# A new written order for the start of attention and a feed-forward layer, with head 18 in it

## The chip, the cores and the metric

The kernel runs on one core of a Trainium2 chip. The metric is the device time of one execution in microseconds (us). Shown are the median of three timed executions and one profiled execution. Its engines are named as the profile names them: PE is TensorE (PEld its weight loads), DVE VectorE, ACT ScalarE, POOL GpSimd, SP the queue that issues all DMA transfers.

## The reference, cut to what matters

Eight batches of eight heads, 576 tokens of 64 elements. A query sees only keys of a short window behind it (32 keys, plain in heads 0 to 3 of a batch, every fourth key in heads 4 to 7). The attention's output, 4608 tokens of 512, goes through two matrices with a clipped square between them.

```
scores = scale * np.matmul(q, k.transpose(0, 1, 3, 2))
scores = np.where(masks, scores, -1e9)
attn = np.exp(scores - max) ; attn = attn / (sum + 1e-09)
x = np.matmul(attn, v)                    # heads side by side: 4608 x 512
h = x @ w_in                              # 512 -> 2048
g = np.where(h >= 1, h, np.where(h <= -1, 0.0, (h + 1) ** 2 / 4))
return g @ w_out                          # 2048 -> 512
```

## The kernel before

A head's 576 queries are six tiles of 96, each with a band of 128 keys. Tokens go through the feed-forward layers in nine groups of 512 with sixteen slices of the inner 2048 each, so in 144 steps: step s is a first layer "A" (four parts of three products), an elementwise chain, and a second layer "B" (four parts of three products). B runs two steps behind A. Products of 512 columns are made of a high and a low part, hence three of each.

The first batch and a half (heads 0 to 17, steps 0 to 17) stand in a table, `OPENING`: a list of tokens that `play` (L588) turns into one instruction or a few each. On each engine and on SP the instructions keep the order of the table. From head 18 and step 18 on a loop makes the order (L642), and it is the same loop before and after. The tokens that matter here:

- `q8`, `k8`, `v8`: loads of queries, keys, values (two heads at a time for heads 0 to 15, one head from head 16 on); `wi3`, `wo3`: loads of a slice of a weight matrix. SP issues them one after the other, and one that waits for its place to come free holds up those behind it.
- `S0.2`: score product of head 0, tile 2 (L287; from head 16 on L302, two tiles, split into high and low parts). Heads 0 to 15 put four tiles, then two, in one PSUM bank.
- `r0.2`: the DVE instruction that adds the mask and takes the row minimum (L263); `m` its mask part from head 16 on (L326). `e0.2`: exponential on ACT (L354), or of a whole head in one instruction after `z`, a subtraction on POOL (L351, L360). Which heads go which way stands in `whole_pass` (L344). `u`, `i`, `R`, `n`: sum, guard, reciprocal, normalisation; `n` runs on POOL or, for the heads in `by_vector`, on DVE (L390).
- `T`, `p`: transposes on PE and their copies; `V`, `x`, `l`: product with the values, its high part (ACT) and low part (DVE).
- `awi3`, `bwi3`, `jwi3`, `hwi3`, `lwi3`: a weight slice is unpacked (a, b on ACT, j on DVE, L188) and split (h on ACT, l on POOL, L199).
- `A4.1`, `B4.1`: products of the layers (L522, L561). `y`, `s`, `j`, `g`, `d`: the chain between them (DVE, ACT, DVE, ACT, DVE). Only two banks hold A's results, so A of a step waits for `d` of the step two before.
- `cq18`, `ck18`, `cs18`, `cl18`: splits of queries and keys of a head from 16 on, on ACT, ACT, DVE and POOL (L217, L220, L224, L228). Raw and split queries and keys have one place each: `q18`'s load waits for `cq17` and `cs17`, `k19`'s for `ck18` and `cl18`, and `cq18` and `ck18` wait for the last score product of head 17.
- `W3`: three products on a constant, to no result.

After the table the loop begins with the score product S18.0, then A of step 18.

Of the kernel before, what the change touches and what calls it, by code (L numbers as in the profile page):

```python
# [60 lines left out]
z8 awi4 wo11 jwo1 A0.2 bwi4 A0.3 lwi3 wi6 e8 S10.0 l6.1.1 y0 hwo1 S11.0 S10.1 S11.1 S10.2 r10.0 wi13 S11.2 s0
r11.0 S10.3 S11.3 r11.1 A1.2 lwo1 r10.1 e11.0 r11.3 r10.2 awi5 j0 wo8 A1.3 e11.1 z9 r10.3 r11.2 g0 S10.4 y1
S11.4 wi8 S10.5 bwi5 S11.5 d0 s1 r10.5 A2.0 r11.4 e11.3 wi10 jwi4 e11.4 A2.1 u8 e9 wo4 A2.2 hwi4 r10.4 jwi5
z10 i8 A2.3 awo2 j1 q14 hwi5 B0.0 R8 u9 g1 B0.1 bwo2 lwi4 k12 d1 B0.2 e11.2 i9 jwo2 e10 B0.3 n8 A3.0 awi7 R9
r11.5 hwo2 y2 A3.1 bwi7 u10 A3.2 s2 n9 A3.3 jwi7 e11.5 i10 B1.0 i11 lwi5 B1.1 j2 hwi7 B1.2 R11 g2 y3 T9.1 lwo2
# [5 lines left out]
V10.1 lwi10 x10.0.0 B4.0 bwo10 l10.0.0 s6 lwi9 jwo10 B4.1 awo8 B4.2 x10.1.1 bwo8 B4.3 j6 awi11 A7.0 l10.1.1
hwo10 jwo8 A7.1 x10.1.0 lwo10 g6 l10.1.0 A7.2 bwi11 d6 hwo8 S12.4 jwi11 S13.4 S12.5 S13.5 awo9 A7.3 lwo8 r13.4
hwi11 r12.5 r12.4 B5.0 r13.5 bwo9 y7 B5.1 lwi11 awi12 jwo9 B5.2 s7 bwi12 S12.0 S13.0 S12.1 S13.1 awo7 r12.0
S12.2 S13.2 r12.1 S12.3 jwi12 S13.3 hwo9 B5.3 q16 r13.0 bwo7 lwo9 j7 A8.0 e13.0 r13.2 g7 jwo7 A8.1 e13.5 A8.2
e13.2 r12.3 awi14 r13.1 A8.3 r12.2 d7 e13.4 z12 B6.0 e13.1 r13.3 y8 bwi14 B6.1 e13.3 jwi14 B6.2 hwo7 i13 e12
# [10 lines left out]
p15.1 S16.0 g14 S16.4 m16.0 A15.0 m16.4 r16.1 A15.1 r16.0 e16.1 d14 S16.2 e16.0 A15.2 r16.4 ck17 m16.2 r16.5
A15.3 cq17 r16.2 cl17 r16.3 e16.2 B13.0 cs17 e16.3 B13.1 e16.4 e16.5 B13.2 k18 i16 V14.1 y15 V14.0 R16 x14.1.1
s15 n16 l14.1.1 B13.3 x14.1.0 j15 x14.0.1 x14.0.0 A16.0 l14.0.1 g15 l14.1.0 A16.1 l14.0.0 t16.1.1 A16.2
t16.0.0 t16.0.1 A16.3 t16.2.1 t16.2.0 t16.1.0 S17.2 B14.0 y16 m17.2 B14.1 s16 d15 B14.2 j16 B14.3 A17.0 g16
# [632 lines left out]
```

## Time and profile before

| what | value |
|---|---|
| median of 3 timed executions | 933.76 us (933.42 to 936.98) |
| the profiled execution's own time | 932.25 us |
| its span in the trace | 930.5 us |
| PE busy | 908.0 us (98%) |
| DVE, ACT, POOL busy | 675.6, 497.4, 233.2 us |
| mean granted PE clock | 0.99 of full |
| chain that ended last | PE 93%, DVE 3%, ACT 2%, DMA 1% |

The span is what the profiler saw from the first to the last instruction; the execution's own time is 1.75 us longer. A busy PE is one with an instruction in it, at whatever clock was granted.

### The profile page before, as it was taken

The numbers are of one execution on the slowest core, as the hardware profiler recorded it, in microseconds if no ns is written. First come the engines' busy times: TensorE is split into PE (matmuls) and PEld (weight loads), VectorE is DVE, ScalarE is ACT, GpSimd is POOL, SyncE is SP. The second block draws the span as 40 slices with busy tenths as digits, with TensorE's granted clock in tenths as the row PEclk, the third lists the DMA queues.
The fourth block names the chain that finished last, engine by engine and source line by source line (L and its number), as shares of the span: only waits on it lengthen the run. The fifth ranks groups of instructions, "written<-read, shape, count | busy, mean of one in ns | idle before, by whom it ended". The sixth has DMA issues, their size and how long they took to land.

```text
span 930.5 us, 14387 instructions
## 1 busy us (share of the span) xinstructions
PE 908.0 (98%) x4856; PEld 743.1 (80%) x4856; DVE 675.6 (73%) x1967; ACT 497.4 (53%) x1372; POOL 233.2 (25%) x150
## 2 busy tenths in 40 slices
PE   8899996999999999999999999999999999999998
PEld 6677885788888888888888888888888888888886
DVE  5998777688888888888887888888888643334333
ACT  6999964455565556555655555555655322222222
POOL 1585542122222222222222222222222000000000
PEclk8999999899999999999999999999999999999999
DMA  9882022122232113222322123222321010001001
GB/s 349 301 331 88 6 74 86 56 70 70 70 115 63 49 57 114 70 70 70 96 89 61 57 67 115 70 70 70 115 69 45 1 46 1 1 1 45 1 1 45
DMA packets 31018, 73.86 MB, mean 79 GB/s; under 512 B 3520, under 2 KB 3808, under 8 KB 30944
## 3 DMA queue, kind: packets, MB, share of 16 engines
q1 hardware_dynamic: 30944, 72.94, 23.6%
q8 instruction: 38, 0.62, 0.3%
q14 instruction: 36, 0.29, 0.1%
HBM read 63.49 MB, written 9.44 MB: 78 GB/s over the span
## 4 chain that ended last, share of the span: by engine, by line
PE 93%; DVE 3%; ACT 2%; DMA 1%; issue 0%; POOL 0%; SPq 0%; DVEq 0%; ACTq 0%
PE acc L561 42%; PE h L522 42%; PE s L302 4%; PE o L456 3%; PE s L287 1%; DVE c_place L263 1%; PE t L432 1%; DVE c L263 0%; DMA msk<-mask_in 0%; DVE xl L497 0%; DMA qr<-q_in 0%; ACT xh L492 0%; DVE wo_m L188 0%; DVE pt L401 0%; DMA out<-out 0%
## 5 line engine op out<-in xcount | busy, mean ns | idle before, releaser
L561 PE MATMUL acc<-wo,gh 128*128 128x512 f32 x1152 | 384.4, 394 | 0.0
L522 PE MATMUL h<-xh,wi 128*128 128x512 f32 x1152 | 358.1, 392 | 0.6 <-DVE gl L549 0.5
L561 PEld LDWEIGHTS acc<-wo,gh 128*128 128x128 f32 x1152 | 216.5, 188 | 47.3
L522 PEld LDWEIGHTS h<-xh,wi 128*128 128x128 f32 x1152 | 210.2, 189 | 39.5 <-DVE gl L549 1.3
L561 PE MATMUL acc<-wo,gl 128*128 128x512 f32 x576 | 225.2, 391 | 0.0
L522 PE MATMUL h<-xl,wi 128*128 128x512 f32 x576 | 225.0, 391 | 0.0
L228 POOL TENSOR_TENSOR kk<-kr,kk 128x608 fp32r<-128x608 f32 x48 | 94.1, 1960 | 425.7 <-ACT kk L220 425.7
L354 ACT ACTIVATE c<-c 96x128 f32<-96x128 f32 x318 | 124.4, 392 | 119.1 <-DVE c L263 118.9
L535 ACT ACTIVATE y<-y,consts 128x512 f32<-128x512 f32 x144 | 104.1, 723 | 125.9 <-DVE y L532 125.7
L545 ACT CAST gh<-h 128x512 fp32r<-128x512 f32 x144 | 84.5, 587 | 121.8 <-PE acc L561 117.5
L532 DVE TENSOR_SCALAR y<-h 128x512 f32<-128x512 f32 x144 | 99.2, 689 | 60.3 <-PE h L522 59.9
L538 DVE TENSOR_TENSOR h<-h,y 128x512 f32<-128x512 f32 x144 | 100.4, 698 | 49.0 <-ACT y L535 47.8
L522 PEld LDWEIGHTS h<-xl,wi 128*128 128x128 f32 x576 | 108.6, 188 | 23.4
L549 DVE TENSOR_TENSOR gl<-h,gh 128x512 fp32r<-128x512 f32 x144 | 98.6, 685 | 38.1 <-ACT gh L545 38.0
L561 PEld LDWEIGHTS acc<-wo,gl 128*128 128x128 f32 x576 | 108.2, 188 | 19.6
L401 DVE STREAM_TRANSPOSE pt<-c 32x192 f32<-32x192 f32 x288 | 106.0, 368 | 8.0 <-POOL c L390 4.7
L390 POOL TENSOR_TENSOR c<-c 96x768 f32<-96x768 f32 x56 | 82.5, 1475 | 31.5 <-DVE c L385 31.4
L326 DVE TENSOR_TENSOR c<-s,msk 96x256 f32<-96x256 f32 (+1 forms) x168 | 61.4, 377 | 37.0 <-PE s L302 36.0
L263 DVE CUSTOM_DVE_ANT_0 c<-s,c 96x128 f32<-96x128 f32 x288 | 70.5, 280 | 1.0
L302 PE MATMUL s<-kk,qs 128*96 128x256 f32 x288 | 57.8, 284 | 8.4 <-DVE qs L224 8.4
L302 PEld LDWEIGHTS s<-kk,qs 128*96 128x96 f32 x288 | 46.2, 162 | 24.1 <-issue 9.0
L354 ACT ACTIVATION_READ_ACCUMULATOR c<-c 96x1 f32 x318 | 59.6, 187 | 0.0
(74 smaller groups left out, 634.2 us busy)
## 6 DMA issues: line engine op xcount, KB each, us to landing
kr<-k_in SPq DMA_DIRECT2D x53, 304.0 KB, 3.1
qr<-q_in SPq DMA_DIRECT2D x53, 288.0 KB, 2.7
vt<-v_in SPq DMA_DIRECT2D x29, 384.0 KB, 3.9
out<-out SPq DMA_DIRECT2D x36, 256.0 KB, 2.1
wi_raw<-w_in SPq DMA_DIRECT2D x16, 512.0 KB, 9.0
wo_raw<-w_in SPq DMA_DIRECT2D x16, 512.0 KB, 8.7
v_place<-v_in SPq DMA_DIRECT2D x3, 384.0 KB, 7.2
k_place<-k_in SPq DMA_DIRECT2D x3, 304.0 KB, 6.6
```

Source lines behind the costliest of these rows:

```text
L228: nc.gpsimd.tensor_tensor(out=kk[:, 1], in0=kr, in1=kk[:, 0].bitcast(F32), op=ALU.subtract)
L302: PE.matmul(out=split_view(n, t0)[:, t - t0], lhsT=hd["qs"][:, t * QT : (t + 1) * QT], rhs=hd["ks"][:, :, t * QT : t * QT + 128], start=Tr ...
L354: nc.scalar.activation(out=c[:, t], in_=c[:, t], func=AF.Exp, bias=st[:, 0, t : t + 1], scale=-1.0, **total)
L390: engine.tensor_tensor(out=c, in0=c, in1=spread(factor(n)), op=ALU.mult)
L401: nc.vector.transpose(out=pts[n % 2][r : r + 32, :, 32 * g : 32 * g + 32], in_=heads[n]["c"][32 * g : 32 * g + 32, :, r : r + 32],)
L522: PE.matmul(out=hps[s], lhsT=ready[f"wi{f}"][:, w, 128 * c : 128 * c + 128], rhs=x[:, c], start=c == 0 and i == 0, stop=c == NC - 1 and i ...
L532: nc.vector.tensor_scalar(out=y, in0=hps[s], scalar1=-1.0, scalar2=1.0, op0=ALU.max, op1=ALU.min)
L535: nc.scalar.activation(out=ys[s], in_=ys[s], func=AF.Square, bias=half_t, scale=0.5)
L538: nc.vector.tensor_tensor(out=hps[s], in0=hps[s], in1=ys.pop(s), op=ALU.max)
L545: nc.scalar.copy(out=gs[s][0], in_=hps[s])
L549: nc.vector.tensor_tensor(out=gl, in0=hps.pop(s), in1=gh.bitcast(F32), op=ALU.subtract)
L561: PE.matmul(out=acc[m], lhsT=g[:, r], rhs=w[:, part], start=f == 0 and i == 0, stop=f == NF - 1 and i == 2,)
```

## The change

The table is written anew. All loads, weight conversions and the order of heads against steps move. A bank's score products now all precede the first minimum taken from that bank; before, they alternated. Head 18's queries are loaded, and split, before the last steps of the table; before, they stood at its very end. Exponentials of heads 4 and 6 become whole passes (with `z4`, `z6` on POOL), head 9's go back to single tiles; `n5` goes from DVE to POOL. There are three constant products less. The mask and the identity matrix for transposes come in one array and one transfer, and the first pair's queries and keys come in halves.

```diff
 OPENING = """
-k0 q0 msk q4 q2 k2 v0 k4 k6 S0.0 q6 S1.0 S0.1 S1.1 r0.0 S0.2 wi0 r0.1 S1.2 e0.0 S0.3 r1.0 S1.3 S0.4 r0.2 wi3
+k0 q0 msk Q0 K0 q2 k2 S0.0 q4 S1.0 S0.1 S1.1 S0.2 k4 S1.2 wi1 S0.3 r0.0 r0.1 e0.0 e0.1 q6 S1.3 r1.0 r1.2 r0.2
...
-S17.0 d16 A17.1 m17.0 A17.2 r17.2 r17.0 e17.2 A17.3 r17.1 r17.3 e17.0 B15.0 e17.1 y17 e17.3 B15.1 s17 B15.2
-j17 B15.3 S17.4 g17 m17.4 ck18 r17.5 r17.4 d17 e17.5 cl18 e17.4 i17 R17 n17 k19 q18 cq18 cs18 q19
+s16 B14.3 j16 S17.2 A17.0 cq18 m17.2 r17.2 A17.1 ck18 r17.3 cs18 g16 A17.2 cl18 e17.2 d16 A17.3 e17.3 B15.0
+i17 y17 B15.1 R17 s17 n17 k19 B15.2 q19 j17 B15.3 g17 d17
 """
-    msk = const.tile([QT, 3, 128], F32, name="msk")
-    ident = const.tile([QT, QT], F32, name="ident")
+    fixed = const.tile([QT, 3 * 128 + QT], F32, name="fixed")
+    msk = fixed[:, : 3 * 128].rearrange("p (k j) -> p k j", k=3)
+    ident = fixed[:, 3 * 128 :]
...
+    first_q, first_k = 3 * QT, 3 * QT + 32
+    whole = {}
+
+    def rest_q(n):
+        nc.sync.dma_start(out=whole["q", n][:, first_q:], in_=q[n // 2][:, first_q:])
+
+    def rest_k(n):
+        nc.sync.dma_start(out=whole["k", n][:, first_k:], in_=k[n // 2][:, first_k:])
...
-            nc.sync.dma_start(out=qr, in_=q[n // 2])
+            some = slice(0, first_q if n == 0 else S)
+            nc.sync.dma_start(out=qr[:, some], in_=q[n // 2][:, some])
+            whole["q", n] = qr
...
-    whole_pass = (8, 9, 10, 12, 14)
-    sum_apart = (4, 5, 6, 7)
-    by_vector = (3, 5, 7)
+    whole_pass = (4, 6, 8, 10, 12, 14)
+    sum_apart = (5, 7)
+    by_vector = (3, 7)
...
         if token == "msk":
-            nc.sync.dma_start(out=msk, in_=mask.rearrange("k p j -> p k j"))
-        elif token == "id":
-            nc.sync.dma_start(out=ident, in_=eye)
+            nc.sync.dma_start(out=fixed, in_=fixed_in)
```

**Where head 18 comes in, on SP.** `kr18`, `qr18` are head 18's raw keys and queries, `out0_0` to `out0_3` the first four results. Before:

```order
L149 DMA kr18_1670<-k2_in 128x608
L574 DMA out<-out0_0_1778 128x512
L574 DMA out<-out0_1_1788 128x512
L574 DMA out<-out0_2_1795 128x512
L574 DMA out<-out0_3_1802 128x512
L149 DMA kr19_1824<-k2_in 128x608
L135 DMA qr18_1826<-q2_in 128x576
L135 DMA qr19_1830<-q2_in 128x576
```

After:

```order
L163 DMA kr18_1649<-k2_in 128x608
L147 DMA qr18_1657<-q2_in 128x576
L588 DMA out<-out0_0_1788 128x512
L588 DMA out<-out0_1_1797 128x512
L163 DMA kr19_1803<-k2_in 128x608
L588 DMA out<-out0_2_1808 128x512
L147 DMA qr19_1811<-q2_in 128x576
L588 DMA out<-out0_3_1817 128x512
```

Head 18's queries moved from behind head 19's keys to right behind its own keys.

**The same place on PE.** `s17_4` and `s17_2` are head 17's score products, `s18_0` head 18's first, `acc0` the second layer, `h1` the first. Before:

```order
L561 MATMUL acc0_3_764<-wo15_1351,gh15_1706 128x512
L561 MATMUL acc0_3_764<-wo15_1351,gl15_1707 128x512
L561 MATMUL acc0_3_764<-wo15_1351,gh15_1706 128x512
L302 MATMUL s17_4_1805<-kk17_1645,qs17_1644 96x256 x2
L302 MATMUL s18_0_1842<-kk18_1813,qs18_1812 96x256 x2
L522 MATMUL h1_2_1848<-xh1_384,wi2_486 128x512 x2
```

After (between the two score products stand the 24 products of A17 and B15, of which four rows are shown):

```order
L316 MATMUL s17_2_1754<-kk17_1615,qs17_1614 96x256 x2
L536 MATMUL h1_1_1757<-xh1_409,wi1_461 128x512 x2
L536 MATMUL h1_1_1757<-xl1_410,wi1_461 128x512
...
L575 MATMUL acc0_3_757<-wo15_1350,gl15_1714 128x512
L575 MATMUL acc0_3_757<-wo15_1350,gh15_1713 128x512
L316 MATMUL s18_0_1834<-kk18_1762,qs18_1761 96x256 x2
L536 MATMUL h1_2_1840<-xh1_409,wi2_522 128x512 x2
```

Before, head 17's last score product stood directly ahead of head 18's first; now a whole step stands between.

**PE at the first pair of heads.** `s0_0` and `s1_0` are the banks of heads 0 and 1, `s2_0` and `s3_0` those of the next pair; what each instruction waits for is in brackets (DVE: a minimum). Before:

```order
L287 MATMUL s0_0_93<-kr0_75,qr0_77 96x128 [waits DMAHW1_49,DMAHW0_49]
L287 MATMUL s1_0_107<-kr0_75,qr0_77 96x128
L287 MATMUL s0_0_93<-kr0_75,qr0_77 96x128
L287 MATMUL s1_0_107<-kr0_75,qr0_77 96x128
L287 MATMUL s0_0_93<-kr0_75,qr0_77 96x128 [waits DVE_49]
L287 MATMUL s1_0_107<-kr0_75,qr0_77 96x128
L287 MATMUL s0_0_93<-kr0_75,qr0_77 96x128 [waits DVE_49]
L287 MATMUL s1_0_107<-kr0_75,qr0_77 96x128 [waits DVE_49]
```

After:

```order
L301 MATMUL s0_0_86<-kr0_74,qr0_76 96x128 [waits DMAHW1_49,DMAHW0_49]
L301 MATMUL s1_0_100<-kr0_74,qr0_76 96x128
L301 MATMUL s0_0_86<-kr0_74,qr0_76 96x128
L301 MATMUL s1_0_100<-kr0_74,qr0_76 96x128
L301 MATMUL s0_0_86<-kr0_74,qr0_76 96x128
L301 MATMUL s1_0_100<-kr0_74,qr0_76 96x128
L301 MATMUL s0_0_86<-kr0_74,qr0_76 96x128 [waits DMAHW4_49,DMAHW3_49]
L301 MATMUL s1_0_100<-kr0_74,qr0_76 96x128
...
L301 MATMUL s2_0_145<-k2_place_83,q2_place_81 96x128 [waits DMAHW5_49,DMAHW6_49,DVE_49,PE_49]
L301 MATMUL s3_0_148<-k2_place_83,q2_place_81 96x128 [waits DVE_49]
```

Within a bank PE no longer waits for DVE; it waits once for the second halves of queries and keys, and at a bank's next pair for the minima of the pair before.

## Rows read from the trace of the kernel before

**Rows 1.** Waits of TensorE (PE), whole trace: us in total, times, longest us.
```profile
...
PE s L302 <- DVE qs L224: 8.4, 1, 8.4
PE s L287 <- DVE c L263: 2.3, 6, 0.7
PE s L287 <- DVE c_place L263: 2.2, 4, 1.0
...
```

**Rows 2.** Windows from:to in us: length, busy us (count) by engine, PEclk, DMA share, GB/s.
```profile
...
6.00:50.70 44.70, 37.35 (x342) 29.61 (x342) 37.51 (x192) 39.33 (x124) 18.29 (x13) 0.92 0.91 346
50.70:155.60 104.90, 103.99 (x588) 83.42 (x588) 86.06 (x201) 84.46 (x200) 56.43 (x40) 1.00 0.28 100
164.00:170.00 6.00, 5.93 (x19) 4.84 (x20) 1.57 (x7) 0.88 (x4) 0.00 (x0) 0.62 0.18 52
176.00:930.50 754.50, 749.98 (x3846) 616.11 (x3840) 539.99 (x1539) 363.98 (x1023) 153.57 (x91) 1.00 0.19 59
...
```

**Rows 3.** Timeline round head 18's first product: start us, us, engine, line, operation, tiles [idle before].
```profile
...
156.67 0.70 ACT L220 CAST kk<-kr 128x608 fp32r<-128x608 f32 x1
...
157.44 1.47 POOL L228 TENSOR_TENSOR kk<-kr,kk 128x608 fp32r<-128x608 f32 x1 [13.91 <-ACT kk L220]
...
158.94 0.34 SPq L149 DMA_DIRECT2D kr<-k_in  x1
...
159.32 4.95 SPq L135 DMA_DIRECT2D qr<-q_in  x2
...
162.46 0.67 ACT L217 CAST qs<-qr 128x576 fp32r<-128x576 f32 x1 [3.81 <-DMA qr<-q_in]
...
164.07 0.71 PE L302 MATMUL s<-kk,qs 128*96 128x256 f32 x2 [8.43 <-DVE qs L224]
...
```

**Rows 4.** Timeline of heads 18 and 19, after the written order.
```profile
...
169.16 0.40 PE L302 MATMUL s<-kk,qs 128*96 128x256 f32 x2
...
172.16 0.40 PE L302 MATMUL s<-kk,qs 128*96 128x256 f32 x2
...
172.84 0.68 ACT L217 CAST qs<-qr 128x576 fp32r<-128x576 f32 x1
...
174.20 2.02 POOL L228 TENSOR_TENSOR kk<-kr,kk 128x608 fp32r<-128x608 f32 x1 [13.78 <-ACT kk L220]
...
179.26 0.40 PE L302 MATMUL s<-kk,qs 128*96 128x256 f32 x2
...
182.24 0.40 PE L302 MATMUL s<-kk,qs 128*96 128x256 f32 x2
...
```

**Rows 5.** Waits of all engines from 0 to 52 us, same columns as rows 1.
```profile
...
DVE c_place L263 <- PE s L287: 3.5, 7, 1.1
...
DVE c L263 <- PE s L287: 1.7, 4, 0.6
...
```

**Rows 6.** Timeline, first products and minima of the opening.
```profile
...
4.90 0.68 PE L287 MATMUL s<-kr,qr 64*96 64x128 f32 x8
...
5.95 0.29 DVE L263 CUSTOM_DVE_ANT_0 c<-s,msk 96x128 f32<-96x128 f32 x1 [5.09 <-DMA msk<-mask_in]
...
```

**Rows 7.** Timeline from 42 us to step 2 of the feed-forward layers.
```profile
...
42.24 1.47 POOL L360 TENSOR_TENSOR c_place<-c_place 96x768 f32<-96x768 f32 x1
...
43.12 2.38 DVE L188 SCALAR_TENSOR_TENSOR wo_m<-wo_m,wo_raw 128x512 uint32<-128x512 uint32 x1
...
43.83 0.89 ACT L351 ACTIVATE c_place<-c_place 96x768 f32<-96x768 f32 x1
...
50.74 0.73 PE L522 MATMUL h<-xh,wi 128*128 128x512 f32 x2 [0.53 <-DVE gl L549]
...
51.03 0.68 DVE L188 SCALAR_TENSOR_TENSOR wi_m<-wi_m,wi_raw 128x512 uint32<-128x512 uint32 x1
...
```

**Rows 8.** Timeline of heads 12 and 13's products.
```profile
...
90.73 0.46 PE L287 MATMUL s<-kr,qr 64*96 64x128 f32 x4 [0.38 <-DVE c L263]
...
```

**Rows 9.** Timeline, exponentials of head 7 in single tiles.
```profile
...
29.97 1.00 ACT L354 ACTIVATE c_place<-c_place 96x128 f32<-96x128 f32 x3
...
```

More of the change, by code (lines that the diff above doesn't have):

```diff
@@ L61 @@
[L61 to L65, printed above, removed]
@@ L71 @@
[L71 to L75, printed above, removed]
@@ L86 @@
[L86 to L89, printed above, removed]
-S17.0 d16 A17.1 m17.0 A17.2 r17.2 r17.0 e17.2 A17.3 r17.1 r17.3 e17.0 B15.0 e17.1 y17 e17.3 B15.1 s17 B15.2
@@ new lines @@
+r4.1 wi4 r2.5 e2.4 R1 r5.3 n1 e2.1 r5.1 wo0 r4.2 e2.5 r3.4 W2 S4.4 r3.5 S5.4 e5.3 S4.5 r4.4 S5.5 q8 e3.1 S6.4
+r5.4 S7.4 S6.5 i2 r4.5 S7.5 e3.3 R2 r5.5 S6.0 z4 e5.0 wo5 r6.4 S7.0 e3.0 r6.5 S6.1 S7.1 r7.5 S6.2 e3.4 S7.2
+S6.3 r6.0 v2 S7.3 r7.4 T1.1 p0.0 r7.0 T0.1 n2 r6.2 T1.0 e5.1 r7.3 e5.2 r7.2 r6.3 e5.5 k8 p0.1 e5.4 r7.1 e3.2
+r6.1 u5 e7.4 W3 T2.1 z6 wo2 e3.5 p1.0 p1.1 i3 e7.5 p2.1 W2 V0.0 i5 e4 wi3 R3 R5 n3 n5 awi0 u4 T3.1 e7.1 V0.1
+e6 p3.1 T2.0 i4 awi1 R4 T3.0 u6 n4 T5.0 x0.1.0 wi13 e7.0 l0.1.0 v6 e7.2 x0.0.0 i6 wo1 R6 e7.3 W3 T4.0 n6
@@ new lines @@
+r8.0 awi4 S10.0 r8.3 S11.0 S10.1 jwo1 S11.1 S10.2 e9.2 S11.2 S10.3 S11.3 awo2 A0.2 r11.0 r11.2 r11.3 e9.3
+r10.1 A0.3 r11.1 e11.2 r10.0 bwo2 r10.2 r10.3 S8.4 S9.4 y0 e11.1 S8.5 S9.5 S10.4 S11.4 e11.3 S10.5 r9.5 S11.5
+A1.2 r11.4 s0 k14 r8.5 r8.4 r10.4 wi11 e11.4 z8 A1.3 j0 e9.1 v8 e11.0 r11.5 wo4 r10.5 g0 y1 wo8 z10 e8 wo11
+r9.4 d0 wo9 s1 u8 wo7 A2.0 bwi4 wo3 A2.1 j1 e9.4 wi12 i8 e9.5 jwi4 A2.2 hwo1 wi8 R8 A2.3 jwo2 n8 i9 e10 R9
+B0.0 y2 hwo2 q12 B0.1 g1 u10 s2 B0.2 n9 d1 wo15 i10 hwi4 B0.3 j2 e11.5 A3.0 lwo1 R10 k12 g2 T9.0 i11 d2 T8.1
@@ new lines @@
+hwo5 l10.0.0 B3.3 s5 lwo5 l10.1.0 A6.0 hwo6 j5 hwi9 A6.1 lwo6 awo7 S12.4 S13.4 g5 S12.5 r12.4 S13.5 A6.2 r13.4
+lwi9 bwo7 r13.5 d5 awi10 A6.3 r12.5 jwo7 bwi10 B4.0 awi11 y6 S12.0 S13.0 S12.1 hwo7 jwi10 S13.1 S12.2 S13.2
+S12.3 bwi11 S13.3 r13.0 B4.1 lwo7 r12.1 k16 s6 r13.1 r13.2 wi14 r13.3 B4.2 e13.5 jwi11 v14 e13.0 B4.3 q14 awo9
+j6 wo14 A7.0 hwi10 q16 r12.3 r12.2 A7.1 r12.0 e13.3 wi15 lwi10 bwo9 A7.2 e13.4 jwo9 hwi11 A7.3 z12 e13.2 B5.0
+g6 y7 B5.1 hwo9 d6 s7 B5.2 lwi11 e12 j7 B5.3 awo8 lwo9 A8.0 u12 g7 A8.1 bwo8 d7 A8.2 i12 awo10 jwo8 A8.3 e13.1
@@ new lines @@
+R12 hwo8 n12 B6.0 y8 awi12 B6.1 i13 bwo10 R13 lwo8 B6.2 s8 jwo10 B6.3 bwi12 n13 A9.0 awi13 j8 hwo10 A9.1 jwi12
+bwi13 A9.2 g8 lwo10 T12.0 d8 T13.1 hwi12 A9.3 p13.1 p12.0 jwi13 B7.0 lwi12 awo12 T13.0 y9 hwi13 T12.1 B7.1
+p13.0 p12.1 bwo12 lwi13 B7.2 s9 jwo12 V12.1 awo11 V12.0 awo15 j9 bwo11 B7.3 v16 x12.1.1 x12.0.1 jwo11 bwo15
+A10.0 l12.0.1 g9 l12.1.1 A10.1 jwo15 x12.1.0 hwo12 A10.2 l12.1.0 x12.0.0 d9 lwo12 hwo11 A10.3 l12.0.0 hwo15
+B8.0 y10 lwo11 awi15 B8.1 s10 S14.4 S15.4 lwo15 S14.5 bwi15 r14.4 S15.5 B8.2 r15.4 r14.5 awo13 r15.5 jwi15
@@ new lines @@
+S16.0 B11.3 m16.0 r16.0 A14.0 r16.1 g13 A14.1 e16.0 d13 e16.1 S16.4 A14.2 m16.4 r16.4 S16.2 r16.5 A14.3 e16.4
+m16.2 e16.5 r16.3 B12.0 ck17 r16.2 y14 V14.1 cq17 cl17 e16.2 V14.0 cs17 e16.3 B12.1 s14 x14.1.1 i16 B12.2
+x14.0.0 k18 x14.0.1 x14.1.0 B12.3 R16 q18 l14.1.1 n16 j14 A15.0 l14.0.1 g14 l14.0.0 A15.1 l14.1.0 t16.2.0
+A15.2 d14 A15.3 t16.1.1 t16.0.0 B13.0 t16.2.1 t16.0.1 t16.1.0 S17.4 B13.1 y15 m17.4 B13.2 s15 B13.3 j15 A16.0
+g15 A16.1 d15 A16.2 S17.0 A16.3 m17.0 r17.1 B14.0 r17.0 e17.1 r17.5 r17.4 e17.0 B14.1 y16 e17.4 B14.2 e17.5
@@ L92, with body @@
+s16 B14.3 j16 S17.2 A17.0 cq18 m17.2 r17.2 A17.1 ck18 r17.3 cs18 g16 A17.2 cl18 e17.2 d16 A17.3 e17.3 B15.0
+i17 y17 B15.1 R17 s17 n17 k19 B15.2 q19 j17 B15.3 g17 d17
 """
 @with_exitstack
-def body(ctx, tc, q, k, q2, k2, v, mask, eye, w_in, w_out, out):
+def body(ctx, tc, q, k, q2, k2, v, fixed_in, w_in, w_out, out):
     nc = tc.nc
@@ L144, in load_k @@
         if n < native:
-            nc.sync.dma_start(out=kr, in_=k[n // 2])
+            some = slice(0, first_k if n == 0 else KPAD)
+            nc.sync.dma_start(out=kr[:, some], in_=k[n // 2][:, some])
+            whole["k", n] = kr
             for j in range(2):
```

52 lines of the change are left out of this document (20 added, 32 removed).

## Prediction

> **What bounds the kernel now.** I read the page first: PE is busy for 98% of the span and makes 93% of the chain that ended last. So the time is PE's work plus the few places where PE stands still or runs at its lower clock, and a change of order can only touch those. The waits of PE [rows 1] name them: one wait of 8.4 us of a score product of the second kind (L302) for a split on DVE, and 4.5 us in ten short waits of the opening's score products (L287) for minima. The windows [rows 2] place them: from 6 to 50.7 us PE is busy for 37.35 of 44.7 us, partly with products on a constant that nobody reads; from 50.7 to 155.6 it lacks only 0.9 us; from 164 to 170 it is busy but was granted 0.62 of its clock; from 176 us to the end it lacks 4.5 of 754.5 us. That last stretch is made by the loop, which the change does not touch, so I give it nothing.
>
> The long wait was read in the timeline [rows 3]. SP holds head 19's keys, which wait for the POOL split of head 18's keys (157.44 + 1.47 = 158.91 us). Head 18's queries stand behind them and go out only at 159.32. ACT splits them at 162.46, DVE after it, and S18.0 starts at 164.07, after 8.43 us without a product. What comes behind is slow: from S18.0 to S18.2 (first layer of step 18 between them) 169.16 - 164.07 = 5.09 us pass, and for the same work one head later 182.24 - 179.26 = 2.98 us [rows 3, 4]. The granted clock, 0.62 on average between 164 and 170 us against 1.00 in the stretches before the pause and after [rows 2], is the reason: PE had stood still for 8 us and then worked for some of that time at the lower of its two levels (1.2 instead of 2.4 GHz).
>
> **The change part by part.**
>
> *Head 18 in the order.* The queries' load now stands right behind the keys' load, ahead of the results and of head 19's keys. It waits for head 17's split, long done by then. The splits of head 18 still wait for head 17's last score product (one place each), but that is now S17.2, and 24 products of A17 and B15 follow before S18.0. Does this cover the splits? Head 19 shows the same pattern: last score product of head 18 at 172.16, ACT's split of the queries at 172.84, POOL's split done at 174.20 + 2.02 = 176.22, S19.0 at 179.26 without a wait [rows 4]. So the splits need 4.1 us; 24 products give close to 2 x 2.98 less a score pair, some 5.6 us. The order puts n16 (POOL, 1.47 us like the pass in [rows 7]) ahead of this split on POOL: if it came late by its whole length, 5.6 us were needed and just covered. I take the whole 8.4 us off, and the 5.09 - 2.98 = 2.1 us of low clock with it. If the cover fails, up to 8.4 + 2.1 come back. On SP, head 19's keys now hold up two results and head 19's queries until POOL is done; the results' readers are none, and those queries are needed a whole head later. Nothing is late next.
>
> *Products before minima, heads 12 and 13.* Two waits of 0.38 us at 89.9 and 90.7 us come from S12 and S13 alternating with minima; one of the two stands in [rows 8]. They lie in the stretch where PE is otherwise full, so they count: 0.8 us.
>
> *Opening, up to step 2.* A2 starts at 50.74 us, when `d0` has freed a bank [rows 7], and PE is full from there on. So the opening is worth what A2 comes earlier; a gain in single waits of PE before that is worth nothing by itself. Up to 50.7 us DVE is idle for 7.2 us and ACT for 5.4 us of 44.7, and the DMA engines have 9% left, 4 us [rows 2]. DVE's waits for score products are 3.5 + 1.7 = 5.2 us [rows 5]; that is the ping-pong which goes. New waits take its place. Four products take 0.68 us and the first minimum starts at 5.95 us now [rows 6]; in the new order it has seven products ahead of it from 4.90 us on, so it starts near 6.1. When the next pair of heads takes the same banks, S3.0 waits for nearly the last minimum of head 1 and six to seven products (1.0 to 1.2 us) pass before the first minimum of head 2, with one or two minima to fill the time; a milder case comes at heads 6 and 7. I put these at 1.9 us, an estimate from the 0.17 us of a product. That leaves 3.3 us on DVE. A0.2 now stands behind the score products of heads 10 and 11, eight of them, 1.4 us, which wait for head 6's last `l`. On ACT, twelve tile exponentials at a third of 1.00 us [rows 9] become two passes of 0.89 [rows 7], 2.2 us less, and head 9 goes the other way, 1.1 us more. Together I take 2.5 us, with 0 and 5.4 us (all of ACT's idle time) as ends: between far ends it is nearest to what DVE keeps, 3.3, less part of the 1.4.
>
> *At nothing.* The halves of the first pair: S0.0 follows the constant products at 4.90 us, without an idle time in its row, so an earlier landing is not seen. The joint transfer of mask and identity lands before 5.95 us if it is no slower than the mask alone, and 6.1 us is when it is needed. Three constant products less lie in time in which PE waits.
>
> *What the change adds on POOL.* Three passes (z4, z6, n5). The row to look at is `jwo1`: 2.38 us at 43.12, while `z8` ran from 42.24 to 43.71 on POOL [rows 7]; the same instruction with no pass beside it took 0.68 at 51.03. So a pass on POOL can cost such a DVE instruction 1.7 us. The Trainium skill, SBUF — State Buffer, section "SBUF: two separate sides", says that DVE and GpSimd share one port pair under an exclusive lock, which a DVE instruction with two SBUF inputs needs for its whole length; the trace agrees with its 2.38 us. By that rule each added pass is a risk for DVE.
>
> **Sum.** 8.4 + 2.1 + 0.8 + 2.5 = 13.8 us. The profiled execution took 932.25 us, so 918.4 for a like one; the median of the three runs is 1.5 us above it, which gives 920.0 us. A measurement of this kernel can tell about 0.5%, 4.7 us, from no change.
>
> **The rivals.**
>
> *POOL blocks DVE in the opening.* For: the 2.38 us above, and three more passes there. Against: minima read a PSUM bank and are short, 0.29 us, and the passes z4 and z6 run among them. Price: 3 x 1.7 = 5.1 us lost where I expect 2.5 gained in all; with the 2.5 left out and 5.1 lost, 932.25 - 11.3 + 5.1 + 1.5 = 927.6 at worst, 922.5 if nothing is lost. By the rule cited above it would be this case; the rows show it for one instruction.
>
> *The wait at head 18 stays.* Only if the POOL split comes late, since the queries are early. Half of it left gives about 925, all of it 930.5. Head 19's row speaks against it.
>
> *The opening gains more.* If ACT's idle time goes altogether and its 1.1 us of saved work too, 6.5 us: 916.
>
> *Slower: the clock in the opening.* If PE idles more before A0.2 with its fewer constant products, the first steps run at the lower level. Price: 2.1 us for each twelve products with their score pair. It has to eat 11.3 us before the kernel is no faster, so five to six such blocks, some 28 us of dense work at the lower level. After the 8.4 us pause the level came back within 5 us [rows 2, 4], which would cost about 2 us. That it lasts is unlikely.
>
> **How the numbers follow.** Chances: the forecast with an opening between 0 and 5.4 us better, 0.60 (917 to 922.5); POOL blocking, 0.20 (922.5 to 927.6); more gain, 0.08 (914 to 917); a wait left at head 18, 0.07 (924 to 930.5); the clock or something like it, 0.05 (from 930 up). Range 915 to 927: it leaves out most of the last two and a little at either end. Faster by over 0.5% means under 929.1: all of the first three and half of the fourth, 0.92. Within 0.5%: 0.05. Slower: 0.03.
>
> **What would show it.** In the new trace PE's list of waits has no line of L302's successor (L316) for a split with more than 1 us, S18.0 follows B15 at once, near 152 us, and the granted clock stays 1.00 round it. No wait of score products for minima near 88 us. A2 starts between 45 and 51 us. POOL's passes stand beside no long `j`. Wrong it is if S18.0 still waits, if A2 starts after 51 us, or if PE is granted less than 1.00 after A0.

## The result, and the profile after

| what | before | after |
|---|---|---|
| median of the timed executions, first comparison | 935.37 us (933.42 to 937.29, 4) | 920.05 us (919.41 to 921.08, 4) |
| the same, in a later comparison | 932.62 us (931.01 to 933.63, 11) | 921.10 us (920.02 to 921.95, 4) |
| the profiled execution's own time | 932.25 us | 921.08 us |
| its span | 930.5 us | 919.3 us |

The ratio after to before was 0.9837, 95% interval [0.9809, 0.9865], in the first comparison and 0.9877 [0.9863, 0.9892] in the later one. Two of the four runs of before in the first had taken 936.98 and 937.29 us, some 4 us more than the rest, and of 28 runs of before in the first two comparisons among the experiments only two were that long (so were two of the six of the first experiment); so 0.9877, or 11.5 us, is the better number, and the spans agree with it: 930.5 - 919.3 = 11.2 us. The median forecast was 920.0; the gain behind it was 13.8 for a profiled execution, so it was 2.6 us too large.

The waits of PE in the changed kernel, whole trace (us in total, times, longest us):

```profile
...
PE o L470 <- DVE xl L511: 2.1, 2, 1.9
PE h L536 <- DVE gl L563: 1.9, 1, 1.9
PE s L301 <- DVE c L277: 1.6, 2, 1.2
PE s L301 <- DVE c_place L277: 1.4, 3, 0.5
...
```

The long wait of [rows 1] is gone, and no wait of a split (L316) is left. The opening's waits for minima fell from 4.5 to 3.0 us. New is one wait of 1.9 us of a first layer (L536) for `d` (`gl`). The wait of 1.9 us in the first line stands ahead of V6, the products with head 6's values; before, PE waited 0.7 us there.

The windows of [rows 2] in the changed kernel, and two more, from 35 to 40 and from 50 to 54 us (length, busy us and count by engine, PEclk, DMA share, GB/s):

```profile
...
6.00:50.70 44.70, 35.73 (x345) 28.77 (x342) 37.37 (x201) 39.61 (x131) 21.23 (x15) 0.92 0.86 324
50.70:155.60 104.90, 104.03 (x588) 83.99 (x587) 81.65 (x197) 84.55 (x202) 57.42 (x42) 0.99 0.31 115
35.00:40.00 5.00, 3.77 (x40) 3.20 (x40) 2.81 (x7) 4.73 (x12) 2.94 (x3) 0.67 0.95 383
50.00:54.00 4.00, 4.00 (x13) 3.10 (x12) 2.13 (x7) 3.46 (x11) 2.54 (x2) 0.57 0.96 346
...
```

Up to 50.7 us DVE, ACT and the DMA engines are about as busy as before, PE less. And PE was granted 0.67 of its clock from 35 to 40 us and 0.57 from 50 to 54, where before it had 1.00 from 30 to 50 us and from 50.7 on [rows 2].

The timeline at head 18, which answers to [rows 3] and [rows 4] (start us, us, engine, line, operation, tiles [idle before]):

```profile
...
149.43 0.40 PE L316 MATMUL s<-kk,qs 128*96 128x256 f32 x2
...
149.86 0.67 ACT L231 CAST qs<-qr 128x576 fp32r<-128x576 f32 x1 [0.26 <-PE s L316]
...
150.44 0.70 ACT L234 CAST kk<-kr 128x608 fp32r<-128x608 f32 x1
...
151.22 1.50 POOL L242 TENSOR_TENSOR kk<-kr,kk 128x608 fp32r<-128x608 f32 x1 [12.42 <-ACT kk L234]
...
151.23 2.11 DVE L238 TENSOR_TENSOR qs<-qr,qs 64x576 fp32r<-64x576 f32 x1
...
155.12 0.40 PE L316 MATMUL s<-kk,qs 128*96 128x256 f32 x2
...
158.09 0.40 PE L316 MATMUL s<-kk,qs 128*96 128x256 f32 x2
...
```

Between S17.2 at 149.43 and S18.0 at 155.12 stand the 24 products of A17 and B15. The splits are done at 153.34, 1.8 us ahead of S18.0, which follows without a wait and at full clock: S18.2 comes 2.97 us later.

The timeline at step 2, which answers to the fourth row of [rows 7]:

```profile
...
49.27 0.73 PE L536 MATMUL h<-xh,wi 128*128 128x512 f32 x2 [1.86 <-DVE gl L563]
...
51.13 1.05 PE L536 MATMUL h<-xh,wi 128*128 128x512 f32 x2
...
52.41 1.05 PE L536 MATMUL h<-xh,wi 128*128 128x512 f32 x2
...
53.69 0.42 PE L575 MATMUL acc<-wo,gh 128*128 128x512 f32 x1
...
```

A2 starts 1.47 us earlier than before, after a pause of 1.86 us, and its later pairs take 1.05 us instead of 0.61: the granted clock from 51 to 53 us was 0.50, its lower level. So its twelve products need 4.42 us, where before they needed 2.86 (B0.0 stood at 53.60 there). B0.0 starts at 53.69, 0.1 us later than before. What the opening had won was gone by then.

### The profile page after: what moved, and what is told of

The parts are those of the page before. It is cut to its first block, busy times and chain, and to the rows that moved or that the text cites. A ratio compares the mean times of both kernels' runs of the same rounds, so it can differ in the third digit from the quotient of the medians.

```text
span 919.3 us, 14389 instructions
## 1 busy us (share of the span) xinstructions
PE 904.1 (98%) x4850; PEld 741.3 (81%) x4850; DVE 669.0 (73%) x1965; ACT 495.7 (54%) x1373; POOL 235.3 (26%) x152
## 4 chain that ended last, share of the span: by engine, by line
PE 93%; ACT 4%; DVE 2%; issue 1%; DMA 0%; DVEq 0%; ACTq 0%
PE acc L575 42%; PE h L536 41%; PE s L316 4%; PE o L470 4%; PE s L301 2%; DVE c_place L277 1%; PE s L262 0%; ACT wi_raw L198 0%; DVE wi_m L202 0%; ACT wi_m L192 0%; PE t L446 0%; DVE c L277 0%; ACT wo_raw L198 0%; ACT wi L209 0%; ACT xh L506 0%
## 5 line engine op out<-in xcount | busy, mean ns | idle before, releaser
L536 PE MATMUL h<-xh,wi 128*128 128x512 f32 x1152 | 357.7, 392 | 1.9 <-DVE gl L563 1.9
L536 PEld LDWEIGHTS h<-xh,wi 128*128 128x128 f32 x1152 | 209.7, 189 | 40.4 <-DVE gl L563 2.3
L536 PE MATMUL h<-xl,wi 128*128 128x512 f32 x576 | 225.0, 391 | 0.0
L536 PEld LDWEIGHTS h<-xl,wi 128*128 128x128 f32 x576 | 108.6, 189 | 23.3
L340 DVE TENSOR_TENSOR c<-s,fixed 96x256 f32<-96x256 f32 (+1 forms) x168 | 61.4, 377 | 34.7 <-PE s L316 33.7
L316 PEld LDWEIGHTS s<-kk,qs 128*96 128x96 f32 x288 | 46.4, 161 | 15.6
L316 PE MATMUL s<-kk,qs 128*96 128x256 f32 x288 | 57.7, 283 | 0.0
```

The costliest lines, as they stand in the source:

```text
L316: PE.matmul(out=split_view(n, t0)[:, t - t0], lhsT=hd["qs"][:, t * QT : (t + 1) * QT], rhs=hd["ks"][:, :, t * QT : t * QT + 128], start=Tr ...
L536: PE.matmul(out=hps[s], lhsT=ready[f"wi{f}"][:, w, 128 * c : 128 * c + 128], rhs=x[:, c], start=c == 0 and i == 0, stop=c == NC - 1 and i ...
```

## The experiments

Nine edits ran, and the changed kernel once more, in three comparisons that each had runs of before beside them. All spans and starts in one place, from the profiled execution of each (A2's pause is the idle time in the row of its first product, A2 to B0 what its twelve products took; in "after, again" and "POOL back" the low clock reached into B0, and from A2's start to A3's all five kernels with over 4 us in this column take 7.2 us, the others 5.6):

| kernel | A2 starts | its pause | A2 to B0 | S18.0 starts | its wait | span | ratio to before |
|---|---|---|---|---|---|---|---|
| before | 50.74 | 0.53 | 2.86 | 164.07 | 8.43 | 930.5 | 1 |
| after | 49.27 | 1.86 | 4.42 | 155.12 | 0 | 919.3 | 0.9837 [0.9809, 0.9865] |
| after, again | 49.23 | 1.86 | 4.02 | 155.15 | 0 | 919.3 | 0.9877 [0.9863, 0.9892] |
| before + head 18 | 50.52 | 0.53 | 2.85 | 155.52 | 0 | 921.5 | 0.9918 [0.9899, 0.9936] |
| after - head 18 | 48.45 | 1.90 | 2.86 | 162.76 | 8.02 | 928.6 | 0.998 [0.9964, 0.9996] |
| after, product last | 47.88 | 1.90 | 4.45 | 157.77 | 3.88 | 923.6 | 0.9924 [0.9907, 0.9941] |
| after, clock kept | 51.41 | 0.30 | 2.85 | 155.75 | 0 | 921.1 | 0.9883 [0.9866, 0.9899] |
| before + bank order | 48.09 | 0.53 | 2.90 | 160.31 | 8.47 | 927.4 | 0.9962 [0.995, 0.9974] |
| after, POOL back | 47.78 | 1.88 | 4.13 | 153.66 | 0 | 917.8 | 0.988 [0.9858, 0.9901] |
| after, loads back | 48.95 | 1.88 | 4.45 | 154.81 | 0 | 919.1 | 0.9879 [0.9865, 0.9892] |
| before + both parts | 48.13 | 0.53 | 2.87 | 151.81 | 0 | 916.1 | 0.9842 [0.9829, 0.9855] |
| after, short pause | 47.21 | 0.92 | 2.86 | 155.30 | 0 | 919.5 | 0.9901 [0.9878, 0.9925] |

**Head 18 alone, put into the kernel before.** The table's stretches that change (in the second, the minima and exponentials of head 17 move up with their products):

```diff
-B13.2 k18 i16 V14.1
+B13.2 k18 q18 i16 V14.1
...
-S17.0 d16 A17.1 m17.0 A17.2 r17.2 r17.0 e17.2 A17.3 r17.1 r17.3 e17.0 B15.0 e17.1 y17 e17.3 B15.1 s17 B15.2
-j17 B15.3 S17.4 g17 m17.4 ck18 r17.5 r17.4 d17 e17.5 cl18 e17.4 i17 R17 n17 k19 q18 cq18 cs18 q19
+S17.0 A17.0 m17.0 g16 S17.4 d16 A17.1 cq18 m17.4 r17.0 A17.2 ck18 r17.1 cs18 cl18 e17.2 r17.5 r17.4 A17.3
+e17.3 e17.0 B15.0 e17.1 y17 e17.5 B15.1 s17 e17.4 B15.2 i17 j17 R17 n17 k19 B15.3 g17 d17 q19
```

> The kernel before, with one part of the change: head 17's last score product (S17.4) moves from the end of the table to just ahead of A17.1, the load of head 18's queries moves from behind head 19's keys to right behind head 18's own keys, and the four splits of head 18 move in behind S17.4. Everything up to step 16 stays. Theory (head 18 is nearly all of the gain): the wait of 8.4 us and the 2.1 us of low clock behind it go, so the time falls by 10.5 us, ratio to before 0.9887, span near 920.0; S18.0 starts near 153.6 instead of 164.07 without a wait, since 21 products (4.9 us) cover splits that took 4.1 us in the row of head 19. Rival (the new opening is a good part of the gain): the time falls by 8 us or less, ratio 0.992 or more. Second rival (the splits come late behind other work on POOL and DVE): a wait of 1 to 3 us is left at S18.0 and the clock drops once more behind it, ratio near 0.993.

The wait and the low clock are gone and the span is 9.0 us shorter; the medians are 9.2 us apart (932.92 and 923.72), while the ratio, 0.9918, makes 7.7 us of it, at the edge of the rival's 0.992. Its timeline (PE) shows why it is not 10.5:

```profile
...
155.52 0.40 PE L301 MATMUL s<-kk,qs 128*96 128x256 f32 x2
...
166.69 0.72 PE L455 MATMUL o<-pt,vt 128*64 128x96 f32 x12 [1.45 <-DVE c L262]
...
```

S18.0 follows B15 at 155.52. Ten microseconds later the product with head 17's values waits 1.45 us for DVE, a wait that neither before nor after has. 9.0 + 1.45 = 10.45: in the profiled execution the forecast's price for head 18, 8.4 + 2.1, holds. The start at 153.6 that I had expected was a slip: the products ahead of S18.0 are those of before, where PE was through with them at 164.07 - 8.43 = 155.64, so it can't come much sooner.

**Head 18 taken out of the changed kernel.**

```diff
-B12.3 R16 q18 l14.1.1
+B12.3 R16 l14.1.1
...
-S17.2 A17.0 cq18 m17.2 r17.2 A17.1 ck18 r17.3 cs18 g16 A17.2 cl18 e17.2 d16 A17.3 e17.3 B15.0
-i17 y17 B15.1 R17 s17 n17 k19 B15.2 q19 j17 B15.3 g17 d17
+A17.0 g16 A17.1 d16 A17.2 A17.3 B15.0 y17 B15.1 s17 B15.2 j17 B15.3 S17.2 g17 m17.2 ck18 r17.2 r17.3
+d17 e17.2 cl18 e17.3 i17 R17 n17 k19 q18 cq18 cs18 q19
```

> The kernel after, with head 18 put back as before: its queries' load behind head 19's keys, head 17's last score product (S17.2) and head 18's splits at the end of the table. The new opening stays. Theory (head 18 is nearly all): the long wait returns with its low clock, 10.5 us, so the span is near 929.8 (from 919.3), ratio to before 0.999. Rival (the opening gains what was forecast, 2.5 + 0.8 us): span near 927, ratio 0.9965, and the wait is not longer than 8.4 us.

The span goes back up by 9.3 us, to 928.6. Its timeline at head 18:

```profile
...
154.34 0.40 PE L315 MATMUL s<-kk,qs 128*96 128x256 f32 x2
...
157.32 0.34 SPq L162 DMA_DIRECT2D kr<-k_in  x1
...
157.71 5.26 SPq L146 DMA_DIRECT2D qr<-q_in  x2
...
162.76 0.71 PE L315 MATMUL s<-kk,qs 128*96 128x256 f32 x2 [8.02 <-DVE qs L237]
...
167.36 0.40 PE L315 MATMUL s<-kk,qs 128*96 128x256 f32 x2
...
```

The wait is back at 8.02 us, and S18.2 follows S18.0 after 4.60 instead of 2.97 us: 8.02 + 1.63 = 9.65. All the rest of the change, in this execution, was worth 930.5 - 928.6 = 1.9 us; by the runs 0.2% with an interval from 0.04 to 0.36%. The runs differ with the clock they were granted: a span of 927.0 us at 0.996, of 932.3 at 0.985. In the profiled one neither of the two pauses of 1.9 us, ahead of V6 and of A2, was followed by half clock, but most of that lead went into a wait of 1.58 us for a copy on ACT at 71.74 us.

**Only the product last.** The load of the queries stays early; head 17's last product and the splits go to the end.

```diff
-S17.2 A17.0 cq18 m17.2 r17.2 A17.1 ck18 r17.3 cs18 g16 A17.2 cl18 e17.2 d16 A17.3 e17.3 B15.0
+A17.0 g16 A17.1 d16 A17.2 A17.3 B15.0 y17 B15.1 s17 B15.2 j17 B15.3 S17.2 g17 m17.2 cq18 ck18 r17.2 r17.3 cs18 cl18
...
```

> The kernel after, in which head 17's last score product and head 18's splits go to the end of the table, while the load of head 18's queries stays early. It parts the two causes of the long wait. If the late load alone made it (the queries behind head 19's keys on SP, as the forecast told it), S18.0 waits 1 us at most and the time stays within 1 us of after, ratio to before near 0.984. If the place of the last product counts by itself, ACT's two splits (0.7 us each), then POOL's (1.5 us) come after it and S18.0 waits 3 to 4 us; a pause of 1.9 us was followed by a half clock for 3 us in the opening of after, so 1.5 to 2 us of low clock are added: 5 to 6 us, span near 925, ratio 0.990.

```profile
...
153.49 0.40 PE L315 MATMUL s<-kk,qs 128*96 128x256 f32 x2
...
155.54 1.47 POOL L241 TENSOR_TENSOR kk<-kr,kk 128x608 fp32r<-128x608 f32 x1 [18.11 <-ACT kk L233]
...
156.02 1.60 DVE L237 TENSOR_TENSOR qs<-qr,qs 64x576 fp32r<-64x576 f32 x1
...
157.77 0.48 PE L315 MATMUL s<-kk,qs 128*96 128x256 f32 x2 [3.88 <-DVE qs L237]
...
162.39 0.40 PE L315 MATMUL s<-kk,qs 128*96 128x256 f32 x2
...
```

So the long wait had two causes in a row. With the load early and the product late, 3.88 us of wait and 4.62 - 2.97 = 1.65 us of low clock are left, 5.5 of some 10 us. The late load makes the other half on top of it; the late load with the product early was not run. The forecast described both moves, but told the wait as the load's alone.

**The clock kept at step 2.** Seven products on the constant more, ahead of A2.0, into a bank that nothing uses then.

```diff
-wo7 A2.0 bwi4
+wo7 X7 A2.0 bwi4
...
+        "X": lambda times: spin(times, ps.tile([128, TOK], F32, tag="acc3", name="more", bufs=1)),
```

> The kernel after, with seven products on the constant more (into a bank that nothing uses then), ahead of A2.0, where TensorE waits 1.86 us for step 0's d. Six such products took 1.53 us at full clock, so seven fill the gap and no more. Theory (the half clock from 50.3 to 53.4 us comes of that pause and eats what the opening won): the granted clock stays 1.00, A2's twelve products take 2.9 instead of 4.4 us, B0.0 starts near 52.2 instead of 53.69 and the span is 1.5 us shorter, near 917.8. Rival (step 2 is paced by something else, the weights' loads at a DMA share of 1.0 or the chain of steps 0 and 1): the clock may stay up but a wait appears behind A2, and the span stays within 0.5 us of 919.3.

The clock stays up in its timeline, the time does not show it:

```profile
...
49.38 1.72 PE L261 MATMUL more<-consts 128*128 128x128 f32 x14
...
51.41 0.73 PE L535 MATMUL h<-xh,wi 128*128 128x512 f32 x2 [0.30 <-DVE gl L562]
...
54.26 0.39 PE L574 MATMUL acc<-wo,gh 128*128 128x512 f32 x1
...
```

With the pause filled, A2's products ran at full clock, 2.85 us. But in this execution the opening ran late before the edit has any part in it: A1 starts at 42.17 us, 2.1 us later than in the changed kernel. The granted clock shows why (windows from 25 to 30 us, the changed kernel first, then this one):

```profile
...
25.00:30.00 5.00, 4.83 (x57) 4.28 (x56) 4.93 (x13) 5.00 (x15) 3.51 (x3) 1.00 0.98 372
...
```

```profile
...
25.00:30.00 5.00, 5.00 (x34) 4.78 (x35) 4.74 (x14) 3.81 (x11) 3.07 (x3) 0.50 0.67 216
...
```

At half clock PE fell from 0.75 us behind the changed kernel (24.41 against 23.66) to 3.5 us behind (33.85 against 30.32). The runs (0.9883 against 0.9877 for the changed kernel) show no gain. Inconclusive for the time. That the clock at A2 hangs on the pause is made likely, not shown: with head 18 taken out the whole pause was there, 1.90 us, and the clock stayed up too.

**The bank order alone, put into the kernel before.** For heads 0 to 15, all products of a bank ahead of its first minimum; nothing else moves.

```diff
-S0.0 q6 S1.0 S0.1 S1.1 r0.0 S0.2 wi0 r0.1 S1.2 e0.0 S0.3 r1.0 S1.3 S0.4 r0.2 wi3
+S0.0 q6 S1.0 S0.1 S1.1 S0.2 S0.3 r0.0 wi0 r0.1 S1.2 e0.0 S1.3 r1.0 S0.4 r0.2 wi3
...
```

> The kernel before, with one part of the change: for heads 0 to 15 a bank's score products are all written ahead of the first minimum from that bank. Nothing else moves. Theory of the forecast: the minima's ping-pong with the products goes, DVE saves 5.2 us of waits and gets back 1.9, the two waits of 0.38 us at heads 12 and 13 go; step 2's first layer starts up to 2.5 us earlier (48.2 instead of 50.74) and the wait at head 18 begins up to 3.3 us earlier; ratio near 0.9965. Rival (the waits only change places, since the bank's next products now wait for its last minimum, and ACT and the loads pace the rest): step 2 starts at 50 to 51.5 us, 0.8 us or less is gained, ratio 0.999 to 1.000. Second rival: each pair's first minimum starts later by six products, 0.4 us and more for each of four pairs, and nothing is given back: step 2 starts after 51.5 us.

```profile
...
48.09 0.74 PE L521 MATMUL h<-xh,wi 128*128 128x512 f32 x2 [0.53 <-DVE gl L548]
...
50.99 0.39 PE L560 MATMUL acc<-wo,gh 128*128 128x512 f32 x1
...
160.31 0.71 PE L301 MATMUL s<-kk,qs 128*96 128x256 f32 x2 [8.47 <-DVE qs L223]
...
165.94 0.52 PE L301 MATMUL s<-kk,qs 128*96 128x256 f32 x2
...
```

A2 starts 2.65 us earlier, where the forecast's term was 2.5, and S18.0 3.76 us earlier behind the same wait. The low clock behind the wait cost 0.5 us more than in before (5.63 instead of 5.09 us to S18.2), so the span is 3.1 us shorter. In the kernel before, this part alone gives what was forecast, and it takes neither the pause nor the half clock at A2 with it.

**The added passes on POOL taken out.**

```diff
-    whole_pass = (4, 6, 8, 10, 12, 14)
-    sum_apart = (5, 7)
-    by_vector = (3, 7)
+    whole_pass = (8, 10, 12, 14)
+    sum_apart = (4, 5, 6, 7)
+    by_vector = (3, 5, 7)
...
-S6.0 z4 e5.0
+S6.0 e5.0
...
-i5 e4 wi3
+i5 e4.0 e4.1 e4.2 e4.3 e4.4 e4.5 wi3
```

> The kernel after, with its three added passes on POOL undone: heads 4 and 6 exponentials again in six single tiles each (no z4, z6), n5 again on DVE. Theory (those passes cost DVE nothing that counts and save ACT 2.2 us): the opening gets later, step 0's clamp (44.9, 44.1, 43.5 in three kernels with this opening) moves to 45 to 47, span 0 to 2 us above the changed kernel's. Rival (a pass on POOL stops DVE's long instructions beside it): the opening gets 1 to 3 us earlier, step 0's clamp starts before 43.5 us, span below the changed kernel's.

The ratio is 0.988 [0.9858, 0.9901], that of the changed kernel. Its opening ran 1.5 us earlier in the profile, but four executions of the new opening with the passes differ among themselves by 1.4 us at A2 (47.88 to 49.27), and the earliest of them is level with this one: ahead of A2 the difference is the clock behind V6, told below. So neither theory is shown; within 0.2% no effect of the passes on the time is seen.

**The first loads as before.**

```diff
-k0 q0 msk Q0 K0 q2 k2 S0.0
+k0 q0 msk q2 k2 S0.0
...
-r0.5 k6 e0.3
+r0.5 id k6 e0.3
```

> The kernel after, with the first loads as before: the first pair's queries and keys whole, the mask in its own transfer, the identity in one of its own behind r0.5. The rest of the new opening stays. Theory of the forecast (at nothing): the first minimum starts where it did (6.3 to 7.5 us in four kernels with the halves), span within 1 us of the changed kernel's. Rival (the halves and the larger joint transfer make the first pairs late: with them TensorE waits 0.4 to 0.8 us for the second halves and 1.2 to 2.5 us before head 2, which no row of before shows): the first minimum starts near 6 us, the thirteenth near 9.6 instead of 9.7 to 11.6, and the opening ends up to 1 us earlier.

Span 919.1 us, ratio 0.9879: the same, as forecast for the time. Its trace does not show that the loads are worth nothing in the opening: three constant products that start at 19.54 us in the changed kernel start at 17.85 here, and the lead goes in the next ten us, in which PE was granted 0.66 of its clock instead of 1.00.

**The two parts together, put into the kernel before.** The bank order, and head 18 as above with head 17's products a little earlier:

```diff
-S17.2 B14.0 y16 m17.2 B14.1 s16 d15 B14.2 j16 B14.3 A17.0 g16 S17.0 d16 A17.1 m17.0
+S17.2 B14.0 d15 y16 m17.2 r17.2 r17.3 B14.1 S17.0 s16 m17.0 B14.2 j16 e17.2 r17.0 r17.1 B14.3 S17.4 A17.0 cq18
...
```

> The kernel before with two parts of the change and nothing else: a bank's score products ahead of its minima, and head 18 in the order (its queries' load early, head 17's last score product just ahead of A17, its splits behind it). Head 17's three score products stand a little earlier than in the run with head 18 alone, since there a wait of 1.45 us came up at the product with the values of head 17. Theory (the two parts are all that the change gains, and they add up): 930.5 less 9.0 and 3.1 is 918.4, and 1.5 us less without that wait, so a span of 916 to 918.5, ratio 0.984 to 0.987, S18.0 near 151.8, no half clock at step 2. It would then be as fast as the changed kernel or up to 3 us faster, since there step 2 starts after a pause of 1.9 us and runs at half clock. Rival (the parts take the same idle time, or the rest of the new order is worth something): span 919 or more, ratio 0.988 or more.

```profile
...
146.04 0.45 PE L301 MATMUL s<-kk,qs 128*96 128x256 f32 x2 [0.35 <-DVE c L262]
...
148.16 0.76 DVE L223 TENSOR_TENSOR qs<-qr,qs 64x576 fp32r<-64x576 f32 x1
...
148.75 1.54 POOL L227 TENSOR_TENSOR kk<-kr,kk 128x608 fp32r<-128x608 f32 x1 [9.04 <-ACT kk L219]
...
151.81 0.40 PE L301 MATMUL s<-kk,qs 128*96 128x256 f32 x2
...
```

S18.0 starts at 151.81, as expected, without a wait. Median 917.82 us, ratio 0.9842 [0.9829, 0.9855], span 916.1: 3.2 us below the changed kernel, whose interval, in another comparison with before, begins at 0.9863. Two parts of the change are worth more than the whole. All four of its executions were granted 0.999 of PE's clock, those of the changed kernel 0.993 to 0.995. And the changed kernel without POOL's passes came to a span of 916.2 us in the one execution that was granted 1.000. So the difference may be the clock's for the most part.

**The pause before A2 shortened in the changed kernel.**

```diff
-S8.4 S9.4 y0 e11.1 S8.5 S9.5 S10.4 S11.4 e11.3 S10.5 r9.5 S11.5 A1.2 r11.4 s0 k14 r8.5 r8.4 r10.4 wi11 e11.4 z8
-A1.3 j0 e9.1 v8 e11.0 r11.5 wo4 r10.5 g0 y1 wo8 z10 e8 wo11 r9.4 d0 wo9 s1 u8
+S8.4 S9.4 S8.5 S9.5 y0 A1.2 e11.1 s0 A1.3 S10.4 S11.4 e11.3 S10.5 S11.5 r9.5 j0 r8.5 g0 r8.4 r9.4 d0 k14 wi11
+z8 e9.1 y1 r11.4 e11.0 v8 r10.4 e11.4 s1 r11.5 wo4 r10.5 wo8 z10 e8 wo11 wo9 u8
```

> The kernel after, reordered at one place: A1.2 and A1.3 stand ahead of the last four score products of heads 10 and 11 instead of behind them, and on DVE and ACT the chain of step 0 (s0, j0, g0, d0) goes ahead of r11.4, r10.4, r11.5, r10.5, y1, e9.1 and e11.0. Theory (the changed kernel's opening loses what the bank order wins to the late d0: 1.1 us of start and 1.5 us of half clock): A2 starts at 48 to 48.5 instead of 49.2, TensorE waits under 1 us there, the clock stays 1.00, B0 starts near 51.2 instead of 53.2 to 53.7, span near 917, ratio 0.985. Rival (the clock falls at this place whatever the pause, or the chain's delay goes to step 1): A3 or B0 waits instead, half clock again, span 919 or more.

The rival came true, one step later (timeline, then the windows view of 55 to 60 us):

```profile
...
47.21 0.73 PE L535 MATMUL h<-xh,wi 128*128 128x512 f32 x2 [0.92 <-DVE gl L562]
...
54.86 0.73 PE L535 MATMUL h<-xh,wi 128*128 128x512 f32 x2 [1.91 <-DVE gl L562]
...
```

```profile
...
55.00:60.00 5.00, 5.00 (x20) 4.01 (x21) 3.19 (x6) 3.55 (x9) 5.00 (x5) 0.66 1.02 417
...
```

A2 starts at 47.21 and runs at full clock. But A3 waits 1.91 us for d1, and the clock falls there. Step 1's chain is the next bound: its clamp starts at 47.07, its `d` at 54.13, and between them stand passes, sums and weight conversions of DVE and ACT that the new order has there. In the changed kernel the same d1 comes at 55.38 and is hidden, because A2 and B0 last until 56.4. S18.0 comes at 155.30, no earlier. The pause was moved, not removed.

## Why the prediction came out as it did

*Head 18, 8.4 + 2.1 us: right.* From before to after S18.0 moved by 164.07 - 155.12 = 8.95 us, of which 8.43 are the wait; from S18.0 to the end after needs 2.25 us less (766.43 and 764.18). Put in alone it gave 9.0 and a new wait of 1.45; taken out, it cost 9.3. The cover that the forecast worked out, 4.1 us of splits under 5.6 us of products, was 3.91 under 5.69.

*Heads 12 and 13, 0.8 us: right, and given back nearby.* From 80 to 100 us PE is busy throughout in the changed kernel. Between 100 and 110 us it now waits 0.9 us in two pieces for copies on ACT (`pt`) in the values of heads 12 and 13, which the forecast did not have.

*The opening, 2.5 us: mis-sized, by all of it.* The step that failed is "A2 starts at 50.74 us, [...] and PE is full from there on. So the opening is worth what A2 comes earlier". A2 came 1.47 us earlier, not 2.5, and full was not full clock: its products took 1.56 us longer, so B0 was 0.1 us later. Both losses are the clock's, which the sum had at nothing in the opening. The first stands behind the pause ahead of V6. From V6's second half to A1, in the changed kernel and in "after, product last", which has the same opening:

```profile
...
36.94 1.23 PE L470 MATMUL o<-pt,v_place 128*64 128x96 f32 x12 [0.26 <-DVE xl L511]
...
38.10 2.02 PE L301 MATMUL s<-kr,qr 64*96 64x128 f32 x16
...
40.05 0.73 PE L536 MATMUL h<-xh,wi 128*128 128x512 f32 x2
...
```

```profile
...
36.94 0.72 PE L469 MATMUL o<-pt,v_place 128*64 128x96 f32 x12 [0.16 <-DVE xl L510]
...
37.59 1.12 PE L300 MATMUL s<-kr,qr 64*96 64x128 f32 x16
...
38.63 0.73 PE L535 MATMUL h<-xh,wi 128*128 128x512 f32 x2
...
```

The same work takes 3.11 us (3.02 in the changed kernel's other trace), or 1.69 to 1.70 in the six traces of the new opening whose clock did not fall there. From A1 to A2 it is 9.2 us in all of these traces but the one with the short pause, so A2 comes 1.3 to 1.4 us later by it. With the same opening and no such fall A2 started at 47.88 and 48.45 us, 2.9 and 2.3 us ahead of before. The price of the minima's ping-pong was about right, as the bank order alone shows (2.65 us), though the clock was not the same there either: before was granted 0.50 from 15 to 21 us, the bank order alone from 16 to 19, the two parts together never, and of the latter two A2 starts at 48.09 and 48.13.

The second loss stands at A2 itself, and its pause comes of the new order. It puts all score products of heads 8 to 11 ahead of A1.2, so nothing is left for PE between A1.3 and A2.0, while `d0` stands behind minima on DVE. The forecast had charged the eight products "part of the 1.4" and had looked at low clock only as the rival that makes the kernel slower, before A0.2, not as a small loss at A2. Shown is that the clock stayed up at A2 in all six traces with a pause of 0.92 us or less there, and in one of six with 1.86 to 1.90 us, and that the two parts without the rest are 3.2 us faster in span. How the 3.3 us between their starts of S18.0 (151.81 and 155.12) divide over the rest of the order was only read from the traces: 1.1 of A2's start (the clock behind V6), 1.5 of A2's clock, 0.9 at heads 12 and 13.

*At nothing: the first loads.* Right for the time (919.1 and 919.3 us). The first minimum came at 6.74 us, not near 6.1, and at 6.15 with the loads as before; what that is worth stays open.

*POOL's passes.* The rival was not seen: no `j` of the opening in the changed kernel takes more than 0.85 us, and without the passes the time is the same. The row behind its price had been read too simply. `jwo1` ended at 43.12 + 2.38 = 45.50 us, long after `z8`; POOL had gone on with a weight split until 44.95:

```profile
...
43.67 1.28 POOL L199 TENSOR_TENSOR wi<-wi_m,wi 128x512 fp32r<-128x512 f32 x1
...
```

So 1.7 us is what two POOL instructions in a row cost it, not one pass. And with `z9` gone POOL has two instructions more up to 50.7 us, not three (13 and 15).

*What would show it.* No wait for a split, full clock round head 18, no wait for minima near 88 us, A2 between 45 and 51: all came. S18.0 near 152 did not (155.12), and the clock below 1.00 after A0 was named as a sign that would make the forecast wrong; it was the sign of the 2.6 us that are missing. That the median still met the forecast's 920.0 is luck: the forecast put the profiled execution at 918.4 and the median 1.5 us above it; they came out at 921.08, and the median 1.0 us below.
